# One 1.5-MB load per expert and an expert-by-expert first chunk in a fused window-attention and maxout-FFN kernel

## The chip, the cores and the metric

The kernel runs on one core of one Trainium2 chip. Times are device microseconds (us) of one execution. A median is that of all executions of a kernel in one job. The profile of a kernel is one such execution, and its span, from the first to the last instruction, is some 1.8 us shorter than the time of the same execution (178.5 against 180.3 us for the kernel before).

## The reference

Inputs are q, k, v of 4 batches, 8 heads, 768 tokens and 64 dimensions in float32; three expert matrices of 512 x 768; and an output matrix of 768 x 512.

```python
def _attn_ref(q, k, v, n_global, n_local):          # n_global 8, n_local 96
    scores = scale * np.matmul(q, k.transpose(0, 1, 3, 2))
    keep = is_global | is_local                     # key < 8, or 0 <= query - key < 96
    scores = scores - slope[h] * dist               # a linear bias on the distance
    a = softmax(np.where(keep, scores, -1e9))
    return np.matmul(a, v)

def _moe_ref(x, w1, w2, w3, w_out):                 # x: the attention result, 3072 x 512
    h = np.maximum(np.maximum(x @ w1, x @ w2), x @ w3)
    return h @ w_out
```

## The kernel before

Tokens go in 24 tiles of 128. A string of units says in which order all work is issued, and with it the order on each engine. The letters that matter here:

- l, v: loads of q and k (0.5 MiB a piece), of v (0.25 MiB). c, C: casts to bf16. x, X: transposes of q and k.
- S: scores, and their exponential on ScalarE. M: multiplication with the mask on VectorE. A: product with v, and scaling. T: transpose of the result. G, V: copies of the eight global keys and values.
- `F c.f.j`: block f (128 of the 768 columns) of expert j for chunk c. A block is four matmuls and its way out of PSUM. O, E: the second matrix and the stores.
- w: a load of expert weights. `W g.j`: cast of column group g (two blocks) of expert j. o, Q: the same for the output matrix. D: three matmuls on zeros as a warm-up.

The last number of a unit often names the engine (0 ScalarE, 1 VectorE, 2 GpSimd).

```python
SCHEDULE = """
    K0 K1 K2 K3 K4 K5 l1.0 l1.1 D0.3 c0.0.2 ...
    M3.0 M3.1 c2.1.2 v3 A1.0 C3.1.0 w0.0 V1.2 x2.1.2 w1.0 A2.1 V2.2 A3.0 T1.0 T2.1 T3.1 W1.0.1 W0.0.0
    G3.2 S4.0.0 S4.1.0 F0.0.0 F0.1.0 M4.0 F0.2.0 F0.3.0 G4.1 S5.0.0 M4.1 S5.1.0 w0.1 W0.1.1 w0.2 W0.2.2
    V3.2 F0.0.1 F0.1.1 F0.0.2 F0.1.2 v4 C4.1.0 A4.0 V4.2 w1.1 W1.1.2 W2.0.0 F0.4.0 F0.5.0 M5.0 M5.1 w1.2
    ... (cut)
"""
    def u_F1(c, f, j):
        W = len(chunks[c]) * 128
        ... (cut)
        ps = psH.tile([128, W], FP32, name="h", tag="h")          # psH: three PSUM buffers
        for dm in range(4):
            nc.tensor.matmul(ps, w123[f // 2][:, dm, j, (f % 2) * 128:(f % 2) * 128 + 128],
                             xT[c][:, dm], start=(dm == 0), stop=(dm == 3))           # L361
        if j == 0:
            h01 = h01_pool.tile([128, W], BF16, name="h01", tag="h01")
            h01s[c, f] = h01
            nc.scalar.copy(h01, ps)                                                   # L366
        elif j == 1:
            nc.vector.tensor_max(h01s[c, f], h01s[c, f], ps)                          # L368
        else:
            nc.vector.tensor_max(ht[c][:, f], h01s[c, f], ps)                         # L370

    def load_w(g, j):                                   # g 0: 256 columns, g 1: 512 columns
        n = 256 * (1 + g)
        st = stage_pool.tile([128, 4, n], FP32, name="wst", tag=f"wst{g}")
        wst[g, j] = st
        nc.sync.dma_start(out=st, in_=wsrc[j][:, 256 * g:256 * g + n].rearrange("(i p) f -> p i f", p=128))

    def cast_w(g, j, how):
        src = wst[0, j] if g == 0 else wst[1, j][:, :, 256 * (g - 1):256 * g]
        copies[how](w123[g][:, :, j], src)                                            # L427
```

The first chunk goes by column blocks here: blocks 0 to 3 of expert 0, then blocks 0 and 1 of experts 1 and 2, then the others. So it can start when a third of one expert is there.

The softmax here doesn't subtract the row's maximum and nothing guards it: scores larger than these inputs give would overflow.

## Time and profile before

| kernel before | value |
|---|---|
| median of three runs | 180.36 us (180.34 to 180.45) |
| span of the profiled run | 178.5 us |
| first matmul of the expert layer (L361) starts | 23.27 us |
| from there to the end of the last output matmul (L376), "the stream" | 151.58 us |
| from there to the end of the span, "the tail" | 3.64 us |

The three parts are my readings of the matmul records. In a timeline a line is a group of like instructions: start, time from first start to last end, engine, line of the program, operation, output<-inputs, shape, count. In brackets stands how long the engine had been idle just before, and what ended that. A waits view has what waited, for what, the total in us, how often, and the longest.

In the waits of TensorE, the one of the expert matmuls:

```profile
PE h L361 <- issue: 0.2, 1, 0.2
```

And the last store in the view of the DMA queue from 174 to 184 us, with its size and the median us from issue to landing:

```profile
out_dram<-ost ACTq DMA_DIRECT2D x1, 64.0 KB, 1.6
```

Behind its first block, before shows no wait for weights on TensorE, and its last store lands 1.6 us after its issue.

### The profile page before, as it was taken

To read this page: it belongs to the slowest core of one execution; us is meant where nothing else is said; L and a number is where in the kernel's file an instruction comes from. 1 tells how busy PE (TensorE), PEld (TensorE's weight loads), DVE (VectorE), ACT (ScalarE), POOL (GpSimd) and SP (SyncE) were. 2 spreads that over 40 slices of the span, in tenths; PEclk is the share of its full clock that TensorE was granted. 3 is DMA by queue.
4 is the path that set the end of the run, shared out by engine and by line. 5 is a ranking of instruction groups with operands and counts; after the bars stand their busy time and mean duration, and the time that the engine had idled before them with its cause. 6 is when DMAs were issued, how large, how long until landed. Compare 5 with 4: busy or idle time off the path is not lost.

```text
span 178.5 us, 3963 instructions
## 1 busy us (share of the span) xinstructions
PE 167.1 (94%) x1529; PEld 95.9 (54%) x1551; DVE 119.1 (67%) x237; ACT 103.2 (58%) x160; POOL 37.4 (21%) x65
## 2 busy tenths in 40 slices
PE   3599799999999999999999999999999999999991
PEld 0455645458866677845555555454454555444451
DVE  4519975977796689748978448978358986137610
ACT  4867898646689958555753936351862543440131
POOL 4255203543343012210006024100020401000000
PEclk9999999999999999999999999999999999999998
DMA  5999999999998899899544999988989664700015
GB/s 139 292 270 243 357 321 383 319 361 356 252 194 229 218 254 227 142 204 234 92 90 122 167 253 231 145 172 152 182 156 300 123 129 147 252 12 4 0 47 190
DMA packets 83587, 35.52 MB, mean 199 GB/s; under 512 B 66160, under 2 KB 78320, under 8 KB 83568
## 3 DMA queue, kind: packets, MB, share of 16 engines
q1 hardware_dynamic: 83424, 35.20, 83.6%
q8 instruction: 12, 0.20, 0.5%
q10 hardware_dynamic: 144, 0.07, 0.1%
q14 instruction: 7, 0.06, 0.1%
HBM read 25.17 MB, written 6.29 MB: 176 GB/s over the span
## 4 chain that ended last, share of the span: by engine, by line
PE 88%; ACT 3%; DVE 2%; POOL 2%; issue 1%; DMA 1%; POOLq 0%; ACTq 0%
PE h L361 53%; PE po L376 16%; PE sp L283 7%; PE op L322 3%; PE op L325 3%; PE tpp L239 3%; PE xtp L349 2%; ACT wmask L300 2%; PE sp L275 2%; DMA out_dram<-ost 1%; DVE qkT L243 1%; DVE xb L332 1%; ACT ost L382 1%; ACT P L288 1%; PE tp L261 1%
## 5 line engine op out<-in xcount | busy, mean ns | idle before, releaser
L361 PE MATMUL h<-xT,w 128*128 128x512 bf16 (+1 forms) x491 | 99.2, 348 | 0.7 <-issue 0.2
L361 PEld LDWEIGHTS <-w 128*128 128x128 bf16 x504 | 47.0, 98 | 40.4 <-ACT w L427 0.2
L288 ACT ACTIVATE P<-sp 128x1024 bf16<-128x1024 f32 (+1 forms) x48 | 43.4, 954 | 20.4 <-PE sp L283 20.2
L368 DVE TENSOR_TENSOR h<-h,h 128x512 bf16<-128x512 bf16 (+1 forms) x42 | 25.2, 609 | 25.6 <-PE h L361 15.5
L366 ACT CAST h<-h 128x512 bf16<-128x512 f32 (+1 forms) x42 | 21.6, 532 | 21.5 <-PE h L361 21.3
L376 PE MATMUL po<-wo,ht 128*128 128x512 bf16 (+2 forms) x147 | 33.1, 362 | 0.5
L370 DVE TENSOR_TENSOR ht<-h,h 128x512 bf16<-128x512 bf16 (+1 forms) x42 | 25.0, 606 | 3.7 <-PE h L361 3.0
L307 DVE TENSOR_TENSOR P<-P,wmask 128x1024 bf16<-128x1024 bf16 x36 | 24.8, 716 | 3.6 <-ACT P L288 3.5
L382 ACT COPY ost<-po 128x512 f32<-128x512 f32 (+2 forms) x20 | 11.2, 564 | 18.4 <-PE po L376 11.2
L376 PEld LDWEIGHTS <-ht 128*128 128x128 bf16 x156 | 14.0, 98 | 13.8
L332 DVE TENSOR_TENSOR xb<-op,rz 128x512 bf16<-128x512 f32 x24 | 16.6, 691 | 0.8
L283 PEld LDWEIGHTS <-qkT 64*128 64x128 bf16 x352 | 10.2, 96 | 10.0 <-issue 8.0
L283 PE MATMUL sp<-qkT 64*128 64x128 bf16 x352 | 15.2, 223 | 0.4 <-DVE xb L332 0.4
L322 PEld LDWEIGHTS <-P 128*128 128x128 bf16 x192 | 12.5, 97 | 2.7 <-ACT P L288 0.2
L221 POOL COPY va<-vaf 8x260 int32<-8x260 int32 x14 | 6.3, 449 | 34.7 <-PE op L325 34.7
L198 POOL CAST qkb<-raw 128x1024 bf16<-128x1024 f32 x7 | 7.2, 1037 | 27.6 <-DMA raw<-in_k_dram 27.6
L322 PE MATMUL op<-va,P 128*128 128x65 bf16 x160 | 12.4, 193 | 0.3 <-ACT va L189 0.2
L239 PE MATMUL tpp<-identb,qkp 128*128 128x128 bf16 x96 | 8.5, 246 | 4.0 <-POOL qkp L183 3.5
L325 PEld LDWEIGHTS <-P 128*128 128x128 bf16 x160 | 10.4, 97 | 1.8 <-issue 0.2
L239 PEld LDWEIGHTS <-qkp 128*128 128x128 bf16 x96 | 7.0, 112 | 5.8 <-POOL qkp L183 4.4
L325 PE MATMUL op<-va,P 128*128 128x65 bf16 x128 | 9.9, 193 | 0.1
L243 ACT COPY qkT<-tpp 128x1024 bf16<-128x1024 bf16 (+1 forms) x9 | 7.9, 873 | 3.4 <-PE tpp L239 3.4
(66 smaller groups left out, 107.7 us busy)
## 6 DMA issues: line engine op xcount, KB each, us to landing
rawv<-in_v_dram SPq DMA_DIRECT2D x24, 256.0 KB, 4.9
out_dram<-ost SPq DMA_DIRECT2D x23, 256.0 KB, 2.3
rawp<-in_q_dram SPq DMA_DIRECT2D x6, 512.0 KB, 7.3
rawp<-in_k_dram SPq DMA_DIRECT2D x6, 512.0 KB, 7.7
wst<-in_moe_w_dram SPq DMA_DIRECT2D x3, 1024.0 KB, 10.3
raw<-in_q_dram SPq DMA_DIRECT2D x12, 256.0 KB, 4.2
raw<-in_k_dram SPq DMA_DIRECT2D x12, 256.0 KB, 4.7
wst<-in_moe_w_dram SPq DMA_DIRECT2D x3, 512.0 KB, 8.6
```

Of the source, the lines that this page charges most:

```text
L239: nc.tensor.transpose(tp[:, e, j - lo], qb["p", n, s][:, e, 2 * j:2 * j + 2].rearrange("i h d -> i (h d)"), identb)
L283: nc.tensor.matmul(sp[:, hh, j2, ds], qT(T - ds, 1)[hsl, jp], qT(T, 0)[hsl, jp], start=not how, stop=True, skip_group_check=True)
L288: nc.scalar.activation(P[:, :, 0:n], sp.rearrange("p a b d n -> p (a b) d n")[:, :, 0:n], AF.Exp, bias=0.0, scale=scale)
L307: nc.vector.tensor_mul(P, P, wmask[:, g, :, 0:2])
L322: nc.tensor.matmul(o, P[:, i, 0], heads(va[T])[:, h], start=True, stop=(t == 0), skip_group_check=True)
L325: nc.tensor.matmul(o, P[:, i, 1], heads(va[T - 1])[:, h], start=False, stop=True, skip_group_check=True)
L332: nc.vector.tensor_tensor(out=x.rearrange("p (g h) d -> p g h d", g=2), in0=o4[:, :, :, 0:64], in1=rz[:, :, :, None].to_broadcast([128, 2, ...
L361: nc.tensor.matmul(ps, w123[f // 2][:, dm, j, (f % 2) * 128:(f % 2) * 128 + 128], xT[c][:, dm], start=(dm == 0), stop=(dm == 3))
L366: nc.scalar.copy(h01, ps)
L368: nc.vector.tensor_max(h01s[c, f], h01s[c, f], ps)
L370: nc.vector.tensor_max(ht[c][:, f], h01s[c, f], ps)
L376: nc.tensor.matmul(po, ht[c][:, f, tt * 128:(tt + 1) * 128], wo[:, f, cols], start=(f == 0), stop=(f == NF - 1))
```

## The change

The intent: fewer and larger loads with longer rows. Each expert comes in one load of 1.5 MB with 3-KB rows, in place of 0.5 and 1 MB with rows of 1 and 2 KB. The first chunk then goes expert by expert over all six blocks, because one expert is there as a whole. That needs six buffers for expert 0's results in place of four. The whole order of units was made anew with it, and the warm-up is gone.

```diff
-    M3.0 M3.1 c2.1.2 v3 A1.0 C3.1.0 w0.0 V1.2 x2.1.2 w1.0 A2.1 V2.2 A3.0 T1.0 T2.1 T3.1 W1.0.1 W0.0.0
-    G3.2 S4.0.0 S4.1.0 F0.0.0 F0.1.0 M4.0 F0.2.0 F0.3.0 G4.1 S5.0.0 M4.1 S5.1.0 w0.1 W0.1.1 w0.2 W0.2.2
-    V3.2 F0.0.1 F0.1.1 F0.0.2 F0.1.2 v4 C4.1.0 A4.0 V4.2 w1.1 ...
+    M2.0 M2.1 v3 C3.1.1 w0.0 M3.0 M3.1 A2.0 w0.1 v4 v5 w0.2 x2.0.2 l3.0 l3.2 V2.2 A3.1 T2.1 c2.1.2
+    x2.1.4 T3.0 W0.0.1 S4.0.0 S4.1.1 F0.0.0 G4.2 S5.0.0 S5.1.0 W1.0.2 V3.1 F0.1.0 F0.2.0 W2.0.2 F0.3.0
+    F0.4.0 F0.5.0 W1.1.0 l3.1 l3.3 M4.0 M4.1 W2.1.0 W0.2.2 v6 v7 C4.1.1 W0.1.1 M5.0 M5.1 C5.1.0 W1.2.0
+    c3.0.2 A4.1 c3.2.2 F0.0.1 F0.1.1 ...
 (the rest of the order is re-made too: cut)
-    h01_pool = ctx.enter_context(tc.tile_pool(name="h01", bufs=4))
+    h01_pool = ctx.enter_context(tc.tile_pool(name="h01", bufs=6))
 def load_w(g, j):
-        n = 256 * (1 + g)
-        st = stage_pool.tile([128, 4, n], FP32, name="wst", tag=f"wst{g}")
-        wst[g, j] = st
-        nc.sync.dma_start(out=st, in_=wsrc[j][:, 256 * g:256 * g + n].rearrange("(i p) f -> p i f", p=128))
+        st = stage_pool.tile([128, 4, DFF], FP32, name="wst", tag="wst")
+        wst[j] = st
+        nc.sync.dma_start(out=st, in_=wsrc[j].rearrange("(i p) f -> p i f", p=128))
 def cast_w(g, j, how):
-        src = wst[0, j] if g == 0 else wst[1, j][:, :, 256 * (g - 1):256 * g]
-        copies[how](w123[g][:, :, j], src)
+        copies[how](w123[g][:, :, j], wst[j][:, :, 256 * g:256 * (g + 1)])
```

(The output matrix takes its staging from the same buffers now. In the changed kernel the cast of weights is L426, and all lines up to there keep their numbers.)

More of the change, by code (lines that the diff above doesn't have):

```diff
@@ L25 @@
 SCHEDULE = """
-    K0 K1 K2 K3 K4 K5 l1.0 l1.1 D0.3 c0.0.2 B0.1 B1.1 B2.1 B3.0 K6 B4.1 B5.1 c0.1.1 c1.0.2 x0.0.4 B6.1
-    B7.1 x0.1.4 S0.0.1 v0 l2.0 l2.1 K7 S0.1.1 G0.0 S1.0.1 S1.1.0 x1.0.3 c1.1.2 M0.0 M0.1 M1.0 v1 x1.1.4
-    C0.1.2 v2 A0.1 G1.2 S2.0.1 M1.1 c2.0.2 x2.0.1 C1.1.1 S2.1.0 G2.2 S3.0.1 M2.0 M2.1 C2.1.1 T0.1 S3.1.1
-    M3.0 M3.1 c2.1.2 v3 A1.0 C3.1.0 w0.0 V1.2 x2.1.2 w1.0 A2.1 V2.2 A3.0 T1.0 T2.1 T3.1 W1.0.1 W0.0.0
-    G3.2 S4.0.0 S4.1.0 F0.0.0 F0.1.0 M4.0 F0.2.0 F0.3.0 G4.1 S5.0.0 M4.1 S5.1.0 w0.1 W0.1.1 w0.2 W0.2.2
@@ L31 @@
-    V3.2 F0.0.1 F0.1.1 F0.0.2 F0.1.2 v4 C4.1.0 A4.0 V4.2 w1.1 W1.1.2 W2.0.0 F0.4.0 F0.5.0 M5.0 M5.1 w1.2
-    W1.2.2 v5 W2.1.0 T4.0 F0.2.1 F0.3.1 l3.0 l3.2 F0.4.1 l3.1 c3.0.2 c3.2.2 F0.5.1 o2 C5.1.0 A5.1 l3.3
-    F0.2.2 Q2.2 F0.3.2 W2.2.0 o0 T5.0 F0.4.2 o1 F0.5.2 x3.0.0 F1.0.0 F1.1.0 c3.1.1 F1.2.0 x3.2.0 Q0.2
-    F1.0.1 F1.1.1 F1.2.1 l4.0 l4.1 c3.3.0 F1.0.2 F1.1.2 F1.2.2 x3.1.2 x3.3.1 F1.3.0 F1.4.0 Q1.2 F1.3.1
-    S6.0.0 S6.1.0 v6 v7 v8 G6.0 F1.3.2 F1.5.0 v9 c4.0.1 F1.4.1 S7.0.0 S7.1.0 G7.2 v10 M6.0 M6.1 M7.0
@@ L36 @@
-    M7.1 O0.0.0 F1.4.2 c4.1.1 C6.1.2 C7.1.2 L12 F1.5.1 S8.0.0 S8.1.0 x4.0.0 O0.1.0 A6.0 x4.1.2 A7.1 V7.2
-    F1.5.2 v11 T6.0 O0.2.0 T7.1 G8.2 C8.1.2 S9.0.0 S9.1.0 G9.1 v12 v13 O0.3.0 F2.0.0 F2.1.0 S10.0.0 M8.0
-    M8.1 M9.0 M9.1 S10.1.0 C9.1.2 L13 L14 F2.0.1 F2.1.1 F2.0.2 A8.0 C12.0.1 F2.1.2 G10.2 O1.0.0 V8.2
-    A9.1 X12.1 M10.0 M10.1 C10.1.0 C11.1.0 F2.2.0 S11.0.0 S11.1.0 M11.0 M11.1 L15 F2.3.0 F2.4.0 O1.1.0
-    V9.2 A10.1 F2.2.1 V10.2 T8.0 F2.3.1 F2.5.0 T9.0 A11.1 F2.4.1 T10.0 F2.2.2 F2.3.2 T11.1 F2.4.2
@@ L41 @@
-    S12.0.0 S12.1.0 F2.5.1 C13.0.2 C14.0.2 C15.0.1 X13.4 F3.0.0 F3.1.0 F3.0.1 G12.1 C12.1.0 F3.2.0
-    F3.1.1 F3.2.1 S13.0.0 S13.1.0 F2.5.2 v14 C13.1.0 C14.1.2 M12.0 M12.1 F3.0.2 F3.1.2 X14.4 F3.2.2
-    X15.4 G13.2 M13.0 M13.1 S14.0.0 S14.1.0 F3.3.0 F3.4.0 F3.5.0 M14.0 M14.1 G14.1 A12.0 A13.1 F3.3.1
-    F3.4.1 F3.5.1 S15.0.0 M15.0 S15.1.0 G15.0 v15 V13.2 L16 L17 v16 T12.4 v17 M15.1 O2.0.0 C15.1.0 A14.0
-    V14.2 F3.3.2 F3.4.2 T13.4 F3.5.2 C16.1.0 C16.0.2 X16.3 T14.4 C17.0.2 A15.1 X17.4 O2.1.0 S16.0.0
@@ L46 @@
-    S16.1.0 G16.1 L18 V15.2 L19 T15.1 M16.0 O3.0.0 M16.1 F4.0.0 F4.1.0 F4.0.1 F4.1.1 C18.0.2 L20 C19.0.2
-    A16.1 F4.2.0 F4.3.0 S17.0.0 S17.1.0 F4.2.1 F4.0.2 F4.3.1 v18 M17.0 v19 M17.1 X18.3 X19.4 C20.0.0
-    V16.2 F4.1.2 C17.1.2 O3.1.1 A17.1 F4.2.2 F4.3.2 S18.0.0 M18.0 S18.1.0 M18.1 F4.4.0 T16.4 T17.4
-    F4.4.1 C18.1.2 C19.1.1 F4.4.2 X20.4 G18.1 S19.0.0 S19.1.0 F4.5.0 L21 M19.0 M19.1 v20 F4.5.1 A18.0
-    T18.4 F4.5.2 A19.1 T19.4 V19.1 C21.0.1 X21.4 G19.1 L22 C22.0.2 L23 X22.4 O3.2.1 O3.3.0 O4.0.1
@@ L51 @@
-    S20.0.0 S20.1.0 M20.0 G20.0 O4.1.0 F5.0.0 F5.1.0 F5.2.0 S21.0.0 S21.1.0 G21.2 F5.0.1 F5.1.1 M20.1
-    M21.0 F5.3.0 F5.0.2 F5.1.2 F5.2.1 F5.2.2 v21 C20.1.1 C21.1.2 F5.4.0 S22.0.0 M21.1 S22.1.0 C23.0.0
-    F5.3.1 M22.0 M22.1 F5.5.0 F5.3.2 A20.0 V20.2 G22.2 v22 F5.4.1 X23.4 v23 F5.5.1 T20.4 A21.1 V21.1
-    T21.4 F5.4.2 F5.5.2 S23.0.0 S23.1.0 M23.0 O4.2.0 M23.1 C22.1.2 A22.0 C23.1.0 O4.3.0 V22.2 T22.4
-    A23.1 T23.4 O5.0.1 O5.1.0 O5.2.1 O5.3.0 F6.0.0 F6.1.0 F6.0.1 F6.0.2 F6.2.0 F6.3.0 F6.4.0 F6.1.1
@@ L56 @@
-    F6.2.1 F6.1.2 F6.3.1 F6.4.1 F6.2.2 F6.3.2 F6.5.0 F6.4.2 F6.5.1 F6.5.2 E
+    B0.1 B1.1 B2.1 B3.1 v0 B4.2 l1.0 l1.1 K0 K1 K2 K3 K4 K5 K6 K7 B5.0 c0.0.2 c0.1.1 B6.1 x0.0.2 B7.1
+    x0.1.4 v1 S0.0.1 S0.1.1 G0.2 S1.0.1 c1.0.2 x1.0.3 v2 M0.0 M0.1 S1.1.1 M1.0 C0.1.2 M1.1 A0.0 c1.1.2
+    C1.1.2 l2.0 l2.1 x1.1.4 C2.1.0 A1.1 V1.1 c2.0.1 G1.0 T0.1 S2.0.1 T1.1 S2.1.0 G2.2 S3.0.1 S3.1.1 G3.0
+    M2.0 M2.1 v3 C3.1.1 w0.0 M3.0 M3.1 A2.0 w0.1 v4 v5 w0.2 x2.0.2 l3.0 l3.2 V2.2 A3.1 T2.1 c2.1.2
+    x2.1.4 T3.0 W0.0.1 S4.0.0 S4.1.1 F0.0.0 G4.2 S5.0.0 S5.1.0 W1.0.2 V3.1 F0.1.0 F0.2.0 W2.0.2 F0.3.0
@@ new lines @@
+    F0.4.0 F0.5.0 W1.1.0 l3.1 l3.3 M4.0 M4.1 W2.1.0 W0.2.2 v6 v7 C4.1.1 W0.1.1 M5.0 M5.1 C5.1.0 W1.2.0
+    c3.0.2 A4.1 c3.2.2 F0.0.1 F0.1.1 F0.2.1 V4.1 F0.3.1 F0.4.1 F0.5.1 c3.1.2 c3.3.2 A5.0 T4.0 F0.0.2
+    x3.0.2 W2.2.0 o2 o1 F0.1.2 F0.2.2 Q1.2 l4.0 T5.1 o0 x3.2.2 F0.3.2 x3.1.1 F1.0.0 F1.1.0 C6.1.1 x3.3.2
+    F1.2.0 F0.4.2 S6.0.0 S6.1.0 G6.0 M6.0 M6.1 F0.5.2 S7.0.0 S7.1.0 G7.2 l4.1 F1.0.1 F1.0.2 F1.1.1
+    F1.1.2 F1.3.0 A6.1 F1.2.1 F1.3.1 S8.0.0 S8.1.0 F1.2.2 F1.3.2 Q2.2 c4.0.2 C7.1.2 M7.0 M7.1 F1.4.0
@@ new lines @@
+    G8.2 F1.5.0 S9.0.0 S9.1.0 G9.2 F1.4.1 F1.5.1 F1.4.2 M8.0 v8 L12 L13 v9 Q0.0 c4.1.2 F1.5.2 v10 A7.0
+    C8.1.0 x4.0.4 x4.1.2 O0.0.0 T6.0 M8.1 M9.0 V7.2 C12.0.1 O0.1.0 S10.0.0 L14 S10.1.0 G10.2 v11 M9.1
+    M10.0 O0.2.1 X12.4 T7.1 O0.3.1 A8.0 C13.0.0 C9.1.0 V8.2 T8.4 F2.0.0 F2.1.0 F2.2.0 A9.1 X13.1 V9.2
+    C14.0.0 v12 C10.1.2 F2.0.1 F2.1.1 F2.2.1 S11.0.0 S11.1.0 F2.3.0 F2.4.0 M10.1 M11.0 O1.0.0 X14.0
+    M11.1 A10.1 V10.2 F2.0.2 F2.1.2 F2.2.2 T9.1 C11.1.0 S12.0.0 S12.1.0 G12.0 F2.3.1 F2.4.1 S13.0.0
@@ new lines @@
+    S13.1.0 F2.3.2 T10.0 F2.5.0 F2.4.2 A11.0 G13.2 M12.0 L15 L16 v13 v14 O1.1.1 F2.5.1 C12.1.0 T11.0
+    S14.0.0 S14.1.0 G14.2 F2.5.2 M12.1 M13.0 M13.1 M14.0 M14.1 C13.1.1 C15.0.2 F3.0.0 F3.1.0 F3.2.0
+    X15.4 C16.0.1 X16.4 A12.1 T12.4 F3.3.0 F3.4.0 v15 A13.0 L17 L18 v16 L19 F3.0.1 F3.1.1 F3.2.1 S15.0.0
+    S15.1.0 G15.2 M15.0 O2.0.0 M15.1 F3.0.2 F3.1.2 C14.1.0 V13.2 A14.1 O2.1.0 S16.0.0 M16.0 S16.1.0
+    G16.1 F3.3.1 F3.2.2 F3.3.2 C15.1.2 C17.0.0 V14.2 A15.1 T13.4 T14.4 T15.4 C18.0.2 X17.0 F3.4.1 F3.5.0
@@ new lines @@
+    V15.2 M16.1 C16.1.1 C19.0.2 S17.0.0 S17.1.0 F3.4.2 F3.5.1 F3.5.2 A16.0 X18.4 V16.2 v17 v18 M17.0
+    X19.1 O3.0.0 O3.1.0 O3.2.0 C17.1.2 F4.0.0 F4.0.1 S18.0.0 S18.1.0 F4.0.2 G18.0 F4.1.0 v19 S19.0.0
+    S19.1.0 F4.2.0 F4.3.0 L20 C20.0.2 T16.4 G19.1 M17.1 L21 M18.0 M18.1 M19.0 C18.1.2 F4.4.0 F4.1.1
+    F4.5.0 M19.1 F4.2.1 F4.3.1 X20.4 A17.1 F4.1.2 C19.1.1 F4.4.1 F4.5.1 A18.0 A19.1 F4.2.2 F4.3.2 F4.4.2
+    T17.4 S20.0.0 S20.1.0 F4.5.2 T18.4 T19.4 L22 O3.3.1 F5.0.0 C21.0.1 X21.4 C22.0.0 G20.2 F5.0.1 M20.0
@@ new lines @@
+    M20.1 F5.1.0 F5.2.0 X22.4 F5.1.1 F5.3.0 F5.4.0 S21.0.0 S21.1.0 F5.2.1 F5.3.1 F5.4.1 M21.0 G21.0
+    S22.0.0 v20 L23 v21 v22 S22.1.0 F5.0.2 M21.1 M22.0 F5.5.0 F5.5.1 M22.1 C20.1.2 V19.2 A20.0 V20.2
+    F5.1.2 F5.2.2 F5.3.2 C21.1.0 v23 A21.0 C23.0.0 X23.4 T20.4 T21.4 O4.0.1 V21.2 C22.1.2 A22.1 C23.1.1
+    V22.2 O4.1.1 G22.2 F5.4.2 T22.4 S23.0.0 M23.0 S23.1.0 F5.5.2 O4.2.0 O4.3.0 M23.1 A23.1 T23.4 O5.0.1
+    O5.1.1 O5.2.0 O5.3.0 F6.0.0 F6.1.0 F6.2.0 F6.0.1 F6.1.1 F6.3.0 F6.2.1 F6.3.1 F6.4.0 F6.0.2 F6.1.2
@@ L57 @@
+    F6.2.2 F6.5.0 F6.4.1 F6.3.2 F6.4.2 F6.5.1 F6.5.2 E
 """
@@ L412, in load_w @@
     def load_w(g, j):
-        n = 256 * (1 + g)
-        st = stage_pool.tile([128, 4, n], FP32, name="wst", tag=f"wst{g}")
-        wst[g, j] = st
-        nc.sync.dma_start(out=st, in_=wsrc[j][:, 256 * g:256 * g + n].rearrange("(i p) f -> p i f", p=128))
+        st = stage_pool.tile([128, 4, DFF], FP32, name="wst", tag="wst")
+        wst[j] = st
+        nc.sync.dma_start(out=st, in_=wsrc[j].rearrange("(i p) f -> p i f", p=128))
     def load_wo(i):
-        st = stage_pool.tile([128, 2, DM], FP32, name="wost", tag="wst0")
+        st = stage_pool.tile([128, 4, DFF], FP32, name="wost", tag="wst")
+        st = st.rearrange("p i f -> p (i f)")[:, 0:2 * DM].rearrange("p (i f) -> p i f", i=2)
         wst["o", i] = st
```

## The prediction

> **What bounds the kernel now.** I read the page first, then the stretches, then the timeline of TensorE. The page's busy rows and the chain that ended last:
>
> ```profile
> PE 167.1 (94%) x1529; PEld 95.9 (54%) x1551; DVE 119.1 (67%) x237; ACT 103.2 (58%) x160; POOL 37.4 (21%) x65
> ...
> PE   3599799999999999999999999999999999999991
> ...
> PE 88%; ACT 3%; DVE 2%; POOL 2%; issue 1%; DMA 1%; POOLq 0%; ACTq 0%
> ```
>
> TensorE (PE) is busy in all slices but the first few, and 88% of the chain is PE. VectorE has 59 us free, ScalarE 75. Busy time alone does not tell whether PE streams or waits, so I look at the distance of matmuls in the timeline of PE, around the first block of the expert layer (the matmuls of L361):
>
> ```profile
> 22.35 0.40 PE L349 MATMUL xtp<-identb,xb 128*128 128x128 bf16 x4 [0.58 <-DVE xb L332]
> 22.68 0.62 PE L283 MATMUL sp<-qkT 64*128 64x128 bf16 x16
> 23.27 3.61 PE L361 MATMUL h<-xT,w 128*128 128x512 bf16 x15
> 26.81 0.62 PE L283 MATMUL sp<-qkT 64*128 64x128 bf16 x16
> 27.36 3.63 PE L361 MATMUL h<-xT,w 128*128 128x512 bf16 x16
> ```
>
> Sixteen matmuls of 512 columns in 3.63 us, the last of which lasts 0.38 (row of L361 by form): (3.63 - 0.38) / 15 = 217 ns each, for 512 columns. I went through all start-to-start distances of the trace: from 22.7 us on, none is longer than its columns and the usual change between kinds of matmul explain, except where a record is missing (a distance of exactly two) and at most 0.15 us once near 106 us, marked as issue. So the kernel has two parts: an opening of 23.27 us, in which PE waits for loads and for short chains of attention, and a stream of matmuls without holes from 23.27 us to the tail. Time after the opening can be saved only by less PE work; time in the opening moves the end one for one.
>
> What sets 23.27? The stretches 0 to 23.27 and after show a DMA queue that is never empty in the opening, and the lines of three engines give the landings:
>
> ```profile
> 0.00:23.27 23.27, 16.74 (x208) 10.45 (x209) 14.64 (x41) 17.12 (x28) 9.27 (x23) 1.00 1.07 264
> ...
> 15.00:19.77 4.77, 4.32 (x73) 2.83 (x72) 4.70 (x11) 4.00 (x4) 1.59 (x3) 1.00 1.24 263
> 19.77:23.99 4.22, 3.29 (x63) 2.48 (x61) 2.88 (x8) 3.87 (x5) 0.55 (x2) 1.00 1.06 372
> ```
>
> ```profile
> 19.77 0.62 ACT L189 CAST va<-rawv 128x512 bf16<-128x512 f32 x1 [0.23 <-DMA rawv<-in_v_dram]
> ...
> 22.07 1.05 ACT L427 CAST w<-wst 128x1024 bf16<-128x1024 f32 x1
> ```
>
> ```profile
> 23.99 0.69 DVE L427 CAST w<-wst 128x1024 bf16<-128x1024 f32 x1 [0.78 <-DMA wst<-in_moe_w_dram]
> ```
>
> The fourth load of v lands at about 19.75 us (the cast at 19.77 waited for it); then come 0.5 MiB and 1 MiB of expert 0, the second landing at about 23.96. The 0.5-MiB piece alone is enough for the first block, so its cast ends at 22.07 + 1.05 = 23.12, and PE starts the block at 23.27, just as its attention work is through. The small first piece is what lets it start there.
>
> **What the Trainium skill says.** "TensorE: Matmul & The Clock Gate", section "Back-to-back issue gap": warm matmuls follow each other at N/2.4 + 2.5 ns, 216 for 512 columns. The trace has 217; that is why I call the stretch after 23.27 a full stream. "Perfetto Trace Analysis", section "Identifying the Most-Contended Engine", warns that busy share of matmuls does not measure the distance from the limit; hence the distances, not the 94%. "DMA: Bandwidth & Descriptors", section "Rules for kernel authors", asks for 1 MiB and more per load, and section "Why small descriptors are slow (HBM only)" says each packet has a fixed cost. The trace agrees in direction: 263 GB/s in 15 to 19.77 us, mostly v with rows of 256 B, against 372 in 19.77 to 23.99, weights with rows of 1 and 2 KB. So going to 3-KB rows can gain little more over the latter, whatever the rule says of large loads.
>
> **The change part by part.**
>
> PE work: the counts of both built programs are the same after the opening. 504 matmuls of L361 and 156 of L376 in both; transposes 96 + 52 + 24 = 172 before, 96 + 44 + 32 = 172 after. The three warm-up matmuls at 1.2 us go (1.5 us in which PE has nothing else to do: no gain), and four bias matmuls come, before the first block. So the stream is as long as before: on the scale of the timed runs 180.36 - 23.27 = 157.09 us, tail included.
>
> Loads: the bytes ahead of the weights are the same, six q/k pieces of 0.5 MiB and four v of 0.25 MiB, 4.19 MB. Only their order differs (v earlier), so they are in at about 19.75 again. Then the first load of weights is 1.5 MiB in one, and its semaphore counts only when all of it is there. Those bytes took 4.2 us before (19.77 to 23.99). With 3-KB rows I take 4.1: landing at 23.85 instead of the first piece's landing near 21.2 (19.75 plus a third of 4.2). The first cast is now on VectorE, 0.69 us in place of 1.05 on ScalarE. Handing on costs about 0.04 before the cast and 0.15 to PE (23.12 to 23.27). First block: 23.85 + 0.04 + 0.69 + 0.15 = **24.73 us, 1.46 later than before**. PE stands idle ahead of it, because all attention work that could fill the hole (the scores of the next two tiles) follows it in PE's order, in part.
>
> The chain of attention gets to the same place a little earlier: v of tile 3 at 19.75, its cast 0.42, two rounds of reciprocal and scaling 0.9 each (0.20 + 0.69), the copy of the transpose 0.42, half a copy of q/k 0.69: 23.1; then scores with bias, about 1 us: near 24.2. So loads and chain are nearly level, and mending one alone would not give back 1.46.
>
> Expert by expert: after the first block come the other five of expert 0 (5 x 0.87), with two scores of 0.62 and A of tile 4 of about 0.5: expert 1 is wanted at 24.73 + 0.87 + 0.7 + 4.33 + 0.5 = 31.1. Its 1.5 MiB lands at 23.85 + 4.1 = 27.95; VectorE does the cast behind the cast of v of tile 4, which lands after it, near 29.1: ready at 29.1 + 0.42 + 0.69 = 30.2. Spare: 0.9. Expert 2 is wanted near 37.1 and lands at 27.95 + 2 x 1.15 + 4.1 = 34.35, cast on GpSimd 1.04: 35.4. Spare: 1.7. So the new order makes no new hole after the start. Expert 0 leaves ScalarE one 0.59 copy a block of 0.87, experts 1 and 2 leave VectorE 0.69 a block of 0.87: VectorE is the tighter one, with three PSUM buffers between, but has the attention of two tiles only beside it. Six buffers for expert 0's results, in place of four, are what this order needs, and cost nothing.
>
> Fewer loads: six become three, on a queue that was full; the sum of bytes is the same. A gain of perhaps 0.1 us per load, all behind the start and hidden.
>
> Rest of the schedule: casts, copies and transposes move between engines everywhere, but a stream without holes cannot be improved on. It can only get holes. I allow 0.1 us on balance, the little that the stall near 106 us gives back included.
>
> Sum: 180.36 + 1.46 = 181.82, about **181.9**.
>
> **The rivals.**
>
> 1. The transfer stays hidden: rows of 3 KB make the load clearly faster, or PE finds attention work ahead of the block. For it: PE waits in several places between 12 and 23 us, so the opening is not tight. Against: 372 GB/s is already near what any stretch of this trace moves (366 in the best 5 us), and the order of PE has the same work ahead of the block. It would give 180.3 to 180.8.
>
> 2. VectorE becomes the bound in the first chunk: twelve maxima of 0.69 (experts 1 and 2) come together with masks, scalings and casts. I count some 16 us of VectorE work in the 21 us from the first block on; an unlucky order with three PSUM buffers would stop PE by 0.5 to 2 us: 182.5 to 184.
>
> 3. The new schedule has holes later: a transposing DMA or a late cast on the path where PE waits. The kernel before shows that such a schedule can be free of holes over 150 us, and the order of the new one looks like made in the same way; each hole would be some tenths. 182 to 183.5.
>
> 4. The shortened opening (v earlier, no warm-up matmuls, finer casts) gains 1 to 2 us before the first block. It cannot end it sooner than the weights land, so this gain would be lost in the wait.
>
> **Range and chances.** The first block cannot start before about 24 us unless the load is faster than any of before, and the stream cannot shrink: below 180.5 is unlikely. Above 183.5 needs 1.7 us of holes. Range 180.5 to 183.5. Two per cent is 3.6 us: faster by that would ask for an opening of under 20 us, before the weights are there, 1%; slower by that asks for 2.1 us of new holes beyond the start, 6%; the rest, 93%, within.
>
> **What would show it.** The first L361 matmul at 24.3 to 25.2 us, PE idle for 0.5 us or more just before it, the cast of the weights on VectorE having waited for the DMA; the first load of weights landing near 23.85. Then groups of sixteen matmuls at 217 ns, and from the first block to the end the same stretch as before within 0.5 us. Wrong would be: the first block at 23.3 or sooner (rival 1 or 4), PE waits for VectorE or for w between 25 and 45 us (rival 2), or waits of PE beyond 0.5 us in sum later on (rival 3).

## The result, and the profile after

The changed kernel took **183.23 us** in the median of four runs (182.60 to 183.36). Before took 180.35 us (180.31 to 180.45) in the same rounds. The ratio of after to before is 1.015, with an interval of 1.013 to 1.017. All ratios here are the mean time of one kernel's fast runs over that of the other's of the same rounds, so not quite the ratio of the medians. It is inside 2% and inside the predicted range. The predicted effect was +1.5 us; the measured one is +2.9.

The three parts, from the traces. E0 is a second run of the changed kernel, unedited:

| us | first block | stream | tail | span |
|---|---|---|---|---|
| before | 23.27 | 151.58 | 3.64 | 178.5 |
| after, the run profiled (182.60) | 24.73 | 152.00 | 4.11 | 180.8 |
| after again, E0 (183.28) | 24.77 | 152.65 | 4.09 | 181.5 |

So the 2.3 us of the profiled run are 1.46 at the start, 0.42 in the stream and 0.47 in the tail. E0 has 0.65 more in the stream. The other three runs of the changed kernel were not traced; they are 0.5 to 0.8 us slower than the profiled one.

The page of the changed kernel: slices of TensorE, the chain by engine, and its waits behind the matmuls of L361.

```profile
PE   0598879999999999999999999999999999999990
...
PE 82%; SPq 7%; DMA 7%; issue 1%; ACT 1%; DVE 0%; ACTq 0%
...
L361 PE MATMUL h<-xT,w 128*128 128x512 bf16 (+1 forms) x491 | 99.0, 348 | 1.9 <-DVE w L426 1.1
```

Slices are 4.5 us here. The sixth slice (22.6 to 27.1) is 7 where TensorE of before shows a 9. DMA has gone from 1% to 7% of the chain, and SyncE's queue, which issues the loads, from nothing to 7%. The path to the start now runs through a load.

TensorE around the first block:

```profile
22.70 0.60 PE L275 MATMUL sp<-bias,identb 128*128 128x512 bf16 x2
23.24 0.40 PE L283 MATMUL sp<-qkT 64*128 64x128 bf16 x8
24.73 1.04 PE L361 MATMUL h<-xT,w 128*128 128x512 bf16 x3 [1.10 <-DVE w L426]
25.70 0.51 PE L283 MATMUL sp<-qkT 64*128 64x128 bf16 x12
```

Attention is through at 23.64 (23.24 + 0.40), and TensorE stands for 1.1 us. VectorE has the reason, and the two lines by which expert 1 can be judged:

```profile
23.98 0.69 DVE L426 CAST w<-wst 128x1024 bf16<-128x1024 f32 x1 [1.16 <-DMA wst<-in_moe_w_dram]
...
29.07 0.43 DVE L189 CAST va<-rawv 128x512 bf16<-128x512 f32 x1 [2.76 <-DMA rawv<-in_v_dram]
29.42 0.69 DVE L426 CAST w<-wst 128x1024 bf16<-128x1024 f32 x1
```

The 1.5 MiB landed at 23.95. The cast of its first third starts at 23.98 and the block at 24.73. The cast of expert 1 starts at 29.42 and is done near 30.1, and its first block runs at 31.06: no hole.

The stretches of the changed kernel (columns: length; busy us and count of PE, PEld, DVE, ACT, POOL; granted clock; DMA share; GB/s):

```profile
15.00:19.77 4.77, 4.12 (x64) 2.31 (x62) 3.43 (x10) 3.98 (x6) 0.21 (x1) 1.00 1.17 309
19.77:23.99 4.22, 3.57 (x58) 2.26 (x55) 2.73 (x7) 3.50 (x7) 1.59 (x3) 1.00 1.03 401
```

With 3-KB rows the same 4.22 us moved 401 GB/s, against 372. How much of these 8% the form of the load itself makes is seen in E1: about 2%. And expert 0 as a whole landed at 23.95, and the second piece of it in before at about 23.96. The extra bytes (275 against 267 GB/s up to there) belong to the loads behind.

Further on, one line of the changed kernel's TensorE differs from its kind:

```profile
46.02 0.89 PE L283 MATMUL sp<-qkT 64*128 64x128 bf16 x16
46.84 2.36 PE L361 MATMUL h<-xT,w 128*128 128x256 bf16 x20
```

Sixteen score matmuls take 0.62 us elsewhere. Here the second half waits 0.27 us for a PSUM slot, until the exponential of the tile before has read it. That is most of the 0.42 of the stream. The other 0.15 us was not placed; the number of changes from other matmuls to scores in the stream is the same in both kernels (19).

At the end, the DMA queue from 178 to 180 us:

```profile
q14 instruction: 1, 0.01, 1.3%
issues: line engine op xcount, KB each, median us to landing
out_dram<-ost ACTq DMA_DIRECT2D x1, 64.0 KB, 2.2
```

A packet of 8 KB on a queue of kind "instruction" goes out just as the last store does, and the store takes 2.2 us in place of 1.6. In before the last packet of this queue goes at 170.7, when no store is in flight. So the theory after the first look was: 1.46 us from the load's single completion, 0.27 and small change from the new order, 0.6 in most runs from something near 47 us, and 0.47 from the fetch of a program. The rivals: the start costs nothing by itself (the attention chain is level with it, as the prediction said); the load and the order cannot be told apart; and the 0.6 is noise of the chip.

### The profile page after: what moved, and what is told of

Same layout as the page of the kernel before. It is cut to its first block, busy times and chain, and to the rows that moved or that the text cites. A ratio compares the mean times of both kernels' runs of the same rounds, so it can differ in the third digit from the quotient of the medians.

```text
span 180.8 us, 3975 instructions
## 1 busy us (share of the span) xinstructions
PE 166.4 (92%) x1532; PEld 95.1 (53%) x1552; DVE 119.1 (66%) x233; ACT 104.5 (58%) x159; POOL 38.0 (21%) x66
## 4 chain that ended last, share of the span: by engine, by line
PE 82%; SPq 7%; DMA 7%; issue 1%; ACT 1%; DVE 0%; ACTq 0%
PE h L361 52%; PE po L376 16%; DMA wst<-in_moe_w_dram 6%; PE sp L283 5%; SPq L158 4%; SPq L174 3%; PE op L322 3%; PE op L325 2%; PE tpp L239 1%; DMA out_dram<-ost 1%; PE tp L261 1%; PE xtp L349 1%; DVE w L426 0%; ACT P L288 0%; ACT ost L382 0%
## 5 line engine op out<-in xcount | busy, mean ns | idle before, releaser
L361 PE MATMUL h<-xT,w 128*128 128x512 bf16 (+1 forms) x491 | 99.0, 348 | 1.9 <-DVE w L426 1.1
L361 PEld LDWEIGHTS <-w 128*128 128x128 bf16 x504 | 46.9, 98 | 41.8 <-DVE w L426 1.3
L288 ACT ACTIVATE P<-sp 128x1024 bf16<-128x1024 f32 (+1 forms) x48 | 43.4, 953 | 24.2 <-PE sp L283 24.2
L366 ACT CAST h<-h 128x512 bf16<-128x512 f32 (+1 forms) x42 | 21.4, 533 | 17.7 <-PE h L361 17.4
L307 DVE TENSOR_TENSOR P<-P,wmask 128x1024 bf16<-128x1024 bf16 x34 | 22.9, 693 | 5.1 <-ACT P L288 5.1
L382 ACT COPY ost<-po 128x512 f32<-128x512 f32 (+2 forms) x17 | 9.3, 556 | 20.5 <-PE po L376 19.0
L239 PE MATMUL tpp<-identb,qkp 128*128 128x128 bf16 x96 | 8.0, 234 | 6.7 <-POOL qkp L183 6.4
L183 POOL CAST qkp<-rawp 128x1024 bf16<-128x1024 f32 x10 | 10.5, 1052 | 2.3 <-DMA rawp<-in_k_dram 1.2
L239 PEld LDWEIGHTS <-qkp 128*128 128x128 bf16 x96 | 6.4, 105 | 7.8 <-POOL qkp L183 6.7
L382 DVE COPY ost<-po 128x512 f32<-128x512 f32 (+1 forms) x9 | 5.8, 643 | 6.4 <-PE po L376 6.4
L221 POOL COPY va<-vaf 8x260 int32<-8x260 int32 x13 | 5.6, 430 | 20.5 <-PE op L325 14.5
```

Source lines behind the costliest of these rows:

```text
L239: nc.tensor.transpose(tp[:, e, j - lo], qb["p", n, s][:, e, 2 * j:2 * j + 2].rearrange("i h d -> i (h d)"), identb)
L288: nc.scalar.activation(P[:, :, 0:n], sp.rearrange("p a b d n -> p (a b) d n")[:, :, 0:n], AF.Exp, bias=0.0, scale=scale)
L307: nc.vector.tensor_mul(P, P, wmask[:, g, :, 0:2])
```

## The experiments

Three jobs on three chips; each has its own runs of before, with medians of 180.32, 180.34 and 180.45 us. All kernels gave correct results.

### E0: the changed kernel again

No edit.

> The changed kernel, unchanged, to see what varies between its executions (182.60 to 183.36 us in four, while the kernel before stays within 0.14). Theory A: the part that varies lies in the loads of the opening, then the first expert block starts at another time than 24.73 us in this profile and the span moves with it. Theory B: it lies in the tail, where in the first profile an instruction fetch of 8 KB sat in front of the last store (last matmul to end 4.11 us, 3.64 in the kernel before); then first block and last matmul stay at 24.73 and 176.73 within 0.1. Theory C: a wait in the middle that comes and goes; then the time between first block and last matmul (152.0 us) changes. Median near 183.2.

Measured: 183.39 us (183.21 to 184.31), ratio 1.018 (1.016 to 1.020). The trace caught what the first one did not have. Timeline of all engines of E0 near 46 us:

```profile
46.05 1.65 DVE L309 TENSOR_TENSOR P<-P,wmask 128x512 bf16<-128x512 bf16 x2 [0.53 <-ACT P L288]
...
46.38 1.04 POOL L429 CAST wo<-wost 128x1024 bf16<-128x1024 f32 x1 [4.81 <-DMA wost<-in_moe_w_out_dram]
...
47.62 0.68 DVE L370 TENSOR_TENSOR ht<-h,h 128x512 bf16<-128x512 bf16 x1
...
48.35 0.38 PE L361 MATMUL h<-xT,w 128*128 128x256 bf16 x2 [0.41 <-DVE ht L370]
```

And the same place in the first profile of the changed kernel:

```profile
46.00 0.91 DVE L309 TENSOR_TENSOR P<-P,wmask 128x512 bf16<-128x512 bf16 x2 [0.53 <-ACT P L288]
...
46.83 0.68 DVE L370 TENSOR_TENSOR ht<-h,h 128x512 bf16<-128x512 bf16 x1
...
47.09 1.04 POOL L429 CAST wo<-wost 128x1024 bf16<-128x1024 f32 x1 [5.51 <-DMA wost<-in_moe_w_out_dram]
```

In E0 a piece of the output matrix landed at 46.33 rather than 47.03. GpSimd's cast of it started between VectorE's two mask products, and the two took 1.65 us in place of 0.91. The maximum behind them came 0.8 us later, its PSUM buffer was not free, and TensorE stood for 0.58 us more. In the Trainium skill, "SBUF — State Buffer", section "Who interferes with whom", a VectorE instruction with two SBUF inputs contends with a GpSimd instruction that reads SBUF, and issue order decides which of them blocks. The trace agrees: both inputs of the mask product are in SBUF, and the 0.74 us are lost behind the cast. E5's trace has the collision too (the cast starts at 46.07, the two products take 1.60 us). Whether it happens hangs on a landing 0.7 us earlier or later. The first profile has it not; by their times most other runs have it.

The start of E0 shows a second state, that of the load of tile 3's v:

```profile
20.11 0.77 DVE L189 CAST va<-rawv 128x512 bf16<-128x512 f32 x1 [2.18 <-DMA rawv<-in_v_dram]
...
24.77 1.04 PE L361 MATMUL h<-xT,w 128*128 128x512 bf16 x3 [0.44 <-DVE w L426]
```

This v landed at 20.09, in the first profile at 18.74. TensorE waits 1.41 us for its cast, attention is through at 24.33 and not at 23.64, and the wait for the weights is 0.44 us in place of 1.10. The first block comes at the same time, because expert 0 lands at 24.00 and 23.95.

### E1: expert 0 alone in two pieces

```diff
-        nc.sync.dma_start(out=st, in_=wsrc[j].rearrange("(i p) f -> p i f", p=128))
+        for lo, hi in ((0, 256), (256, DFF)) if j == 0 else ((0, DFF),):
+            nc.sync.dma_start(out=st[:, :, lo:hi], in_=wsrc[j][:, lo:hi].rearrange("(i p) f -> p i f", p=128))
```

> The changed kernel with one thing undone: the first 1.5-MB load in two pieces, columns 0 to 255 and 256 to 767, as in the kernel before. Theory 'the landing of the whole load sets the start': the first piece lands near 20.2 us, the cast on VectorE then waits only for the copies ahead of it (22.82), PE ends the scores at 23.64, and the first block starts at 23.6 to 23.8 in place of 24.73: about 1.0 us less, 182.2. Rival 'the attention chain sets the start': no change, 24.7 and 183.2.

Measured: 182.20 us (182.08 to 182.34), ratio 1.011 (1.009 to 1.012); first block 23.32, stream 153.13, tail 3.99. TensorE of E1:

```profile
23.32 1.04 PE L361 MATMUL h<-xT,w 128*128 128x512 bf16 x3
...
24.94 4.49 PE L361 MATMUL h<-xT,w 128*128 128x512 bf16 x20
30.13 0.20 PE L322 MATMUL op<-va,P 128*128 128x65 bf16 x1 [0.70 <-DVE va L189]
```

The start moves by 1.41 us (24.73 to 23.32), back to where before has it. So the wait at the start is the single completion of the load: shown. In this run, with tile 3's v landing at 18.84, the attention chain was ready for it; in the state of E0 it would have held the start back to 24.33. But 0.86 us by the distance of starts (0.70 as the trace counts idle time) are handed back at 30.13, because A of tile 4, which comes right after expert 0, waits for the fourth tile's v. That v lies behind the whole of expert 1 in the queue and lands at 29.62, 0.57 later than in the first profile (29.05), so the split itself is a part of this wait. E1's stretch, to be read beside those of the other two kernels:

```profile
19.77:23.99 4.22, 3.88 (x56) 2.32 (x54) 3.62 (x8) 3.49 (x6) 1.43 (x3) 1.00 1.05 392
```

With expert 0 in rows of 1 and 2 KB again it is 392 GB/s: 2% under the changed kernel, not 8%. Expert 0 is complete at 24.19 to 24.48 in the six traces with the split, and at 23.92 to 24.26 in the four of this order without it. Whether it is the shorter rows or the additional load that costs this was not separated.

The net is 1.2 us against E0 (183.39 to 182.20), but not all of it comes from the start. E1's trace has no collision near 46 us:

```profile
45.72 0.91 DVE L309 TENSOR_TENSOR P<-P,wmask 128x512 bf16<-128x512 bf16 x2 [0.54 <-ACT P L288]
...
46.86 1.04 POOL L430 CAST wo<-wost 128x1024 bf16<-128x1024 f32 x1 [4.95 <-DMA wost<-in_moe_w_out_dram]
```

Against the first profile, which has none either, E1's span is only 0.4 us shorter (180.8 to 180.4). So about 0.4 of the 1.2 us are what is left of the start, and most of the rest is the missing collision.

### E2: the load alone, in the order of before

```diff
 (on the kernel before: load_w, load_wo and cast_w of the changed kernel; w1.0, w1.1, w1.2 taken out of the order)
```

> The kernel before, with its own order of units, and the weights in three loads of 1.5 MB: the loads alone, without the new order. Theory: the load lands at 23.95, is cast on ScalarE by 25.0, first block at 25.2 (23.27 before), +1.9 us; the third expert is wanted at 31.0 and is ready near 33.3, +2.3: about 184.5 us. Rival 'the loads alone cost only the later start and the order of blocks does not matter': +1.5 to 2, 182.

Measured: 188.59 us (188.24 to 189.97), ratio 1.048 (1.045 to 1.051): worse than either expected number. The first block is at 25.32, the stream 158.09. TensorE stands 2.0 us near 33 for the cast of expert 2, as expected. Then comes a collision that nobody expected; all engines of E2 from 35.9 us:

```profile
36.15 2.01 POOL L426 CAST w<-wst 128x1024 bf16<-128x1024 f32 x2
...
36.70 5.42 DVE L307 TENSOR_TENSOR P<-P,wmask 128x1024 bf16<-128x1024 bf16 x2
...
38.12 2.01 POOL L183 CAST qkp<-rawp 128x1024 bf16<-128x1024 f32 x2
...
40.09 1.49 POOL L429 CAST wo<-wost 128x1024 bf16<-128x1024 f32 x1
...
42.77 0.81 PE L361 MATMUL h<-xT,w 128*128 128x512 bf16 x3 [2.53 <-DVE h L368]
```

Five casts lie on GpSimd back to back from 36.15 to 41.58. VectorE's two mask products, 0.69 us each when alone, took 5.42, and TensorE stood 2.5 us. After that its granted clock was 0.62 from 42.7 to 46.5, which costs another 1.4 us by my count (3.8 x 0.38). (The other five runs have a mean clock of 0.98, the profiled one 0.991, at like times; they were not traced.) Two things follow. In the old order as it stands, the single load costs 8 us: some 4 are the waits that were expected (2.05 at the start, 1.98 for expert 2), some 4 the collision and the clock behind it. In the new order the whole change costs under 3. And the collision of E0 is a small form of this one.

### E3: the piece early, and the first cast on GpSimd

E1, and in the order:

```diff
-    x2.1.4 T3.0 W0.0.1 S4.0.0 S4.1.1 F0.0.0 G4.2 ...
+    x2.1.4 T3.0 W0.0.2 S4.0.0 F0.0.0 S4.1.0 G4.2 ...
```

> The changed kernel with the first load split, the first cast on GpSimd instead of VectorE, and the second scores of tile 4 behind the first block and without bias matmuls. Theory: nothing but the last transposed copy of attention (22.97 us) is then left ahead of the first block: start at 23.0 to 23.2, about 1.6 us less than the changed kernel, 181.6 us. If the start is 23.0 to 23.2 and the time is over 182, a hole has opened later. Rival: no gain beyond that of the split alone.

Measured: 183.01 us (182.42 to 183.51), ratio 1.015 (1.013 to 1.017). A miss. TensorE of E3:

```profile
24.14 1.02 PE L361 MATMUL h<-xT,w 128*128 128x512 bf16 x3 [0.25 <-ACT xT L350]
25.09 0.51 PE L283 MATMUL sp<-qkT 64*128 64x128 bf16 x12
25.86 0.29 PE L283 MATMUL sp<-qkT 64*128 64x128 bf16 x4 [0.26 <-POOL qkT L216]
26.76 0.40 PE L283 MATMUL sp<-qkT 64*128 64x128 bf16 x8 [0.61 <-ACT P L288]
```

With the weights early, the block waits for the transposed attention result instead, and the scores moved behind it find their inputs late. So there the attention chain does come close behind the load: it allows 23.3 in the order of E1, and not less.

### E4: the cast of the output matrix behind the mask products

```diff
-    ... F0.1.2 F0.2.2 Q1.2 l4.0 ...    S7.0.0 S7.1.0 G7.2 l4.1 ...
+    ... F0.1.2 F0.2.2 l4.0 ...         S7.0.0 S7.1.0 G7.2 Q1.2 l4.1 ...
```

> The changed kernel with the first cast of the output weights (GpSimd, 1.04 us) moved one place back, behind the small copy G of tile 7, so that it cannot start before the scores of tile 7 are read. Theory 'collision': in the slower executions this cast starts at 46.4 us, just ahead of VectorE's two mask products, one of which then takes 1.2 in place of 0.42 us, VectorE empties PSUM late and PE stands for 0.58 us at 47.7; in the fastest one the load landed later and the cast started at 47.1, behind them. Then with the move every execution is like the fastest: 182.6 to 182.8 us, about 0.6 less than the changed kernel of this job's neighbours (183.2 to 183.4), and no PE wait for VectorE near 47.7. Rival 'it varies for another reason': median stays at 183.3.

Measured: 182.48 us (182.31 to 184.45), ratio 1.014 (1.011 to 1.017). Five of six runs lie between 182.31 and 182.81, and their mean is 1.012 times that of before; those of E0 lay at 183.2 and above. The trace of E4 is that of the sixth run, so its times are shifted, but the order on the engines can be read:

```profile
47.84 0.91 DVE L309 TENSOR_TENSOR P<-P,wmask 128x512 bf16<-128x512 bf16 x2 [0.54 <-ACT P L288]
...
48.92 2.02 POOL L429 CAST wo<-wost 128x1024 bf16<-128x1024 f32 x2
```

The products take 0.91 again, and the cast starts after them. So some 0.9 us go with the collision, as far as two jobs on two chips can be compared through their runs of before; the traces account for 0.65 of it (152.65 against 152.00).

The sixth run (184.45 us) shows a mode that a run of E0 (184.31) and one of E5 (184.51) have too: clock 0.989 in the mean, where all other runs of the changed kernel and its variants have 0.994 or more. In its trace TensorE stands 1.57 us before the first block, and from 24.73 to 28.00 the granted clock is 0.54. Some 2 us go there. Before never shows it, nor does any run of a variant whose profiled run starts before 24.5 us. Standing longer at the start seems to raise the risk; three runs are too few to show it.

### E5: six small VectorE instructions moved to GpSimd

```diff
-        for tvar in va_ring + va_first:
-            nc.vector.memset(heads(tvar)[:, :, 64:65], 1.0)
 ... (at the end of the set-up)
+        for tvar in va_ring + va_first:
+            nc.gpsimd.memset(heads(tvar)[:, :, 64:65], 1.0)
```

> The changed kernel with the six small memsets of the opening on GpSimd instead of VectorE, which changes nothing but the number of VectorE's instructions (six fewer). Theory 'fetch in the tail': the 8-KB instruction packet at 178.5 us is VectorE's next piece of program, asked for three instructions before its end; with six fewer it is never asked for, and the last store lands sooner: from the last matmul to the end 3.6 to 3.7 us in place of 4.0 to 4.1, time about 0.4 less, 182.8 to 183.0. Rival 'the packet is another engine's': it is still there, tail 4.0 to 4.1, 183.3.

Measured: 182.98 us (182.41 to 184.51), ratio 1.016 (1.013 to 1.019); tail 3.55. The time itself says little, as the collision and the mode of E4 lie in it. The tail is what the run was for. The last store of E5, from the DMA queue from 174 us on:

```profile
out_dram<-ost ACTq DMA_DIRECT2D x1, 64.0 KB, 1.7
```

The instruction packet now goes at 182.5, when the program is over, and the store is back at 1.7 us. With six VectorE instructions fewer the packet came later. GpSimd has six more, which would bring a packet of its own sooner, so I take it for a fetch of VectorE's program. E6 and E10 have the same edit and tails of 3.5; E9, without it, has 4.2. All traces agree: in the eight where this packet goes at most 2.8 us before the end, the tail is 3.99 to 4.26, in the six others 3.43 to 3.64.

### E6 and E10: the known costs mended together, twice

The edits of E1, E4 and E5; the cast of expert 1's first columns ahead of that of tile 4's v, and A of tile 4 two blocks later; and one block moved between the scores of tiles 6 and 7, against the wait of 0.27 us:

```diff
-    ... C4.1.1 W0.1.1 ...   c3.0.2 A4.1 c3.2.2 F0.0.1 F0.1.1 F0.2.1 ...   F0.5.2 S7.0.0 ...
+    ... W0.1.1 C4.1.1 ...   c3.0.2 c3.2.2 F0.0.1 F0.1.1 A4.1 F0.2.1 ...   F0.5.2 F1.0.1 S7.0.0 ...
```

> The changed kernel with all that was found undone at once: first load split (start 23.3 in place of 24.7), the cast of expert 1's first block ahead of the cast of v of tile 4 and A of tile 4 two blocks later (the wait of 0.86 us for that v after the split), the scores of tile 7 one block later (the wait of 0.27 us near 46 us), the two edits of the neighbours. If these terms are the whole difference, it comes to 183.3 - 1.45 - 0.27 - 0.6 - 0.4 = 180.6 us, level with the kernel before. If something else costs time, it stays over 181.5.

> The mended kernel once more, for a second profile: spans went from 179.7 to 180.8 us in six executions. Theory 'the fourth v': the first block starts at either 23.3 or 24.3 and the span follows it. Rival: the start is 24.3 again and the span differs behind it, at a wait that the first profile (1.4 us in sum, all ahead of the start) didn't have, a GpSimd cast beside VectorE's products being the first candidate.

Measured: 182.21 us (181.58 to 182.81), ratio 1.010 (1.009 to 1.012), and, on another chip, 181.76 us (181.49 to 182.21), ratio 1.008 (1.006 to 1.009). Better than the changed kernel by 0.5 to 1% in their ratios to before, but not the 180.6 that I had expected, and still behind before. The first blocks are at 24.34 and 24.43, the streams 151.87 and 151.97, the tails 3.5. The waits of 0.27 and at 47 us are gone: TensorE of E10 is busy in all of 45 to 50 us, against 4.91 of 5.00 in the changed kernel. What did not come is the early start of E1: the first block follows the scores without a wait, and they are late, as in E0. In both traces v of tile 3 landed at 20.0 to 20.2, and in E1 at 18.8. In E6 and E10 a 16-KB instruction packet goes out at 16.9 and 17.3 us, between the loads; in E1 at 18.1, after v. In all ten traces of kernels with this order of loads, a packet before 17.4 goes with a v at 20.0 or later and one after 17.6 with a v at 18.7 to 19.0. E0 and the first profile, of one and the same kernel, are one of each. That is an association, not tested by an edit of its own.

### E8 and E9: where the early start goes

E8 is E1 with A of tile 4 two blocks later (the first two edits above); E9 is E6 without the moved memsets.

> The changed kernel with the first load split and, of the further edits, only that which takes the wait for v of tile 4 away (its cast behind that of expert 1's first block, its product two blocks later). If the mended kernel stayed at 182.2 because of the edits added there, this one gains the 0.86 us of that wait over the split alone: 181.3 to 181.5 us. If something behind the wait takes its place (VectorE is late anyway), it stays at 182.0 to 182.2.

> The mended kernel without the move of the memsets to GpSimd. Theory: the memsets shifted the opening so that the 16-KB instruction packet went in front of the fourth v (landing 20.2 in place of 18.8, first block 24.3 in place of 23.3) and cost more than the 0.45 us that they won in the tail; then v lands at 18.8 here, the block starts at 23.3 and the time is 181.0 to 181.4. Rival: v lands at either time in either kernel; then this one spreads as the mended one did, 181.6 to 182.8, median 182.

Measured: E8 182.42 us (181.99 to 182.66), ratio 1.011 (1.009 to 1.012); E9 182.06 us (181.64 to 182.29), ratio 1.008 (1.007 to 1.010). The first blocks are at 23.68 and 23.34, and the wait for v of tile 4 is gone, yet both missed what I had expected by 0.7 to 0.9 us. E9 from 36 us:

```profile
36.12 1.04 POOL L183 CAST qkp<-rawp 128x1024 bf16<-128x1024 f32 x1 [0.46 <-DMA rawp<-in_q_dram]
...
37.22 0.56 PE L239 MATMUL tpp<-identb,qkp 128*128 128x128 bf16 x7 [0.47 <-POOL qkp L183]
```

The transposes of the next q and k wait for GpSimd's cast, and that for its load. In the changed kernel this cast starts at 35.95, in E1 at 36.29, in E8 at 36.23, in E10 at 36.05: nearly the same, though their first blocks lie between 23.3 and 24.7. The queue delivers at its own pace, and with the split a little later. The scores of tile 6, far behind, start at 44.68 in the changed kernel, and at 44.39, 44.48, 44.22 and 44.46 in E1, E8, E9 and E10. Of the 1.41, 1.05 and 1.39 us that E1, E8 and E9 won at the start, 0.29, 0.20 and 0.46 are left there; E10, which starts 1.1 us after E9, is only 0.24 behind it. This is why mending the start does not give its 1.46 us back.

### E7: before, with v ahead of a piece of k

```diff
 (on the kernel before: v3 ahead of l2.1; T3.1 c2.1.2 W0.0.0 F0.0.0 x2.1.2 W1.0.1 F0.1.0 G3.2 S4.0.0 ... in place of the old order)
```

> The kernel before, with the loads of v of tiles 1 to 3 ahead of the second piece of q/k of tiles 4 and 5, and that piece's transpose and scores behind the first expert block: an attempt to start the block earlier than 23.27. Theory: in that kernel the chain from the fourth v (landing 19.75) sets the start, not the weights (cast by 23.1); v lands about 1.8 us earlier, the weights become the limit (landing 21.2, cast 1.05): start near 22.5, time 179.6 to 180.0. Rival: the delayed scores of tile 4 open holes behind the start, 180.3 or more.

Measured: 184.46 us (183.78 to 185.70), ratio 1.024 (1.021 to 1.027). A miss as an attempt to beat both kernels. The first block starts at 23.04 rather than the 22.5 expected, and the scores and the second group of blocks then find their inputs late: three holes of TensorE between 25 and 30.5 us. The stream is 154.79. Loads put off are asked for again some us later.

### E11: before without the warm-up

```diff
-    ... l1.0 l1.1 D0.3 c0.0.2 ...
+    ... l1.0 l1.1 c0.0.2 ...
```

> The kernel before without its three warm-up matmuls: the one part of the change that takes PE work away. Theory: nothing hangs on them (PE idles from 2.6 to 6.2 us behind them), 180.3 within 0.1, unless six PE instructions fewer let the instruction packet of 16.2 us come later and the fourth v sooner, then up to 0.4 less. Rival: they warm the clock, then the transposes and scores of the opening run longer at half clock and it is up to 0.5 us slower.

Measured: 180.42 us (180.38 to 180.44), ratio 1.000 (0.999 to 1.001). The warm-up is worth nothing, as the prediction said.

| kernel | median us | ratio to before | first block | stream | tail |
|---|---|---|---|---|---|
| E0 after again | 183.39 | 1.018 | 24.77 | 152.65 | 4.09 |
| E1 expert 0 in two pieces | 182.20 | 1.011 | 23.32 | 153.13 | 3.99 |
| E2 load alone | 188.59 | 1.048 | 25.32 | 158.09 | 3.43 |
| E3 cast on GpSimd, scores later | 183.01 | 1.015 | 24.14 | 153.53 | 4.03 |
| E4 cast behind masks | 182.48 | 1.014 | 25.03 | 153.56 | 4.06 |
| E5 memsets on GpSimd | 182.98 | 1.016 | 24.70 | 152.57 | 3.55 |
| E6 mended | 182.21 | 1.010 | 24.34 | 151.87 | 3.51 |
| E7 before, v first | 184.46 | 1.024 | 23.04 | 154.79 | 4.18 |
| E8 two pieces, A later | 182.42 | 1.011 | 23.68 | 152.95 | 4.26 |
| E9 mended, memsets back | 182.06 | 1.008 | 23.34 | 152.76 | 4.20 |
| E10 mended, again | 181.76 | 1.008 | 24.43 | 151.97 | 3.52 |
| E11 before, no warm-up | 180.42 | 1.000 | 23.38 | 151.59 | 3.63 |

(The parts are of the one run profiled; E4's was its slow one.) No version beats the kernel before.

## Why the prediction was right or wrong

- **What bounds the kernel** was right for this change: an opening, then a stream of matmuls, and the later start came through to the end. As a rule, "time in the opening moves the end one for one" was wrong: E1, E8 and E9 start 1.05 to 1.41 us sooner and have 0.20 to 0.46 of it left at the scores of tile 6, because waits for later loads open in the stream.
- **The start** was right to 0.01 us by sum: 24.73 predicted, 24.73 measured. The landing came 0.1 later than predicted (23.95), the handing on to TensorE was short by as much. That the landing came out has some luck in it: tile 3's v landed at 18.74 and not at 19.75, and expert 0 took 5.2 us after it and not 4.1 (in E0 20.09 and 3.9). Only their sum held, in both traces. E1 shows that the single completion makes it.
- **"Loads and chain are nearly level, and mending one alone would not give back 1.46"** was right for one state of the kernel and wrong for the other. Where tile 3's v lands at 20.0 or later (E0, E6, E10), the chain is through at 24.33 to 24.50, close to the predicted 24.2, and in E0 the load alone could give back some 0.4 us (24.77 less 24.33). Where it lands at 18.7 to 18.8 (first profile, E1), the chain is through at 23.4 to 23.6, and E1 gave the start back, 1.41 us. Of that, only about 0.4 us reached the end, for a reason that the prediction had not: later loads set the pace (E1, E8, E9). E3 shows that the chain does hold a still earlier start back.
- **No hole for experts 1 and 2** was right: weights wanted at 31.1 and there; the third expert landed at 34.40 (34.35 predicted), with no wait of TensorE.
- **Rows of 3 KB gain little** was right: 401 GB/s against 392 in E1, where expert 0 has the short rows of before in the new order. They do gain some 0.4 us at the landing of the whole expert 0 over two pieces in this order, but the first block has no use for the whole.
- **The step that failed** is "I allow 0.1 us on balance" for the rest of the order, with the stretch after the start taken over from before, "tail included". In its place stand 0.42 us in the stream (0.27 of them one wait for a PSUM slot), 0 to 0.6 us of a collision on most runs, and 0.47 us in the tail. With 1.46 they make 2.35 to 2.95; measured are 2.25 for the run without the collision and 2.9 in the median. The prediction's own sign fails with it: from the first block to the end it allowed 0.5 us more than before, and it is 0.9 in the first profile and 1.5 in E0. Rival 3 named holes "of some tenths" and gave 182 to 183.5; that is what came. Rival 2 saw that VectorE late with a maximum stops TensorE through PSUM, but looked at VectorE's own load between 25 and 45 us; GpSimd's cast was the cause, at 47.
- **The tail** was not thought of at all. The last fetch of what, by E5, is VectorE's program moved from 170.7 to 178.5 us, and no count of instructions in the prediction would have told where it falls.

Open are: why the output matrix lands at 46.3 in one run and 47.0 in another; the 0.15 us of the stream that was not placed; the 1.2 us between the fastest and the slowest run of E6 (181.58 to 182.81), of which only one was traced; and whether the packet at 17 us makes v late or only goes with it.

## What to carry to other kernels

The cast of a third of expert 0 waited for the last byte of all of it (landing 23.95, cast 23.98). Where the first consumer needs only a part, a small first piece lets it start sooner (E1: 1.41 us), but the loads behind then come some 0.4 us later. No version here gained by the large loads over the kernel before. A start won by an earlier load holds only if the loads behind it come earlier too; look for the next wait for a load before counting the gain. On an engine order without holes, check beside TensorE whether GpSimd casts now lie beside VectorE products of two SBUF inputs, because 0.7 us in a landing then decided over 0.65 us of the whole.

## What the Trainium skill lacked or had wrong

- "Runtime: NRT & Kernel Launch", section "Instruction fetch mechanics", calls the cost of a fetch mostly hidden. "DMA: Bandwidth & Descriptors", section "Queues, rings and completion order", does put such refills on rings of the same 16 engines, but no page says what one costs a store beside it. Here an 8-KB packet beside the last store made it 2.2 us long in place of 1.6, and the tail 0.47 us longer (E5 puts it right); a 16-KB packet near 17 us goes with a v that lands at 20.0 to 20.2 rather than 18.7 to 19.0.
- "DMA: Bandwidth & Descriptors", section "Rules for kernel authors", asks for loads of 1 MiB and more. It has no word on what a large load costs its first reader; "Perfetto Trace Analysis", section "DMA Optimizations", says that splitting may let work start sooner, without a number. Here the single load gained 2% in rate (392 to 401 GB/s, E1 against the changed kernel), and the split let the first block start 1.41 us sooner.
- "SBUF — State Buffer", section "Who interferes with whom", is right on the lock, but gives no size for a run of GpSimd instructions: one cast cost two mask products 0.74 us (0.91 to 1.65), and casts back to back took two of 0.69 us to 5.42 us. It has the second instruction wait until the first finishes; in E2 one product lasted from 36.70 to 40.68, beside four casts.
